# A planned two-layer attention kernel: V's weights split two blocks ahead, K's first weights split during Q in layer B's later units, and another model of loads and ports in the planner

## The chip, the cores and the metric

The kernel runs on one core of a Trainium2 chip. A core has a matrix engine (PE; PEld is its weight load), a vector engine (DVE), a scalar engine (ACT), a general engine (POOL), and SP, which here only issues transfers. They share an on-chip memory of 128 partitions; matrix products land in banks of 128 x 512 float32 values, which DVE or ACT must empty before PE can fill them again. Each engine works through its own queue in order and waits on semaphores for the others. The metric is the time of one launch in microseconds of device time.

## The reference

Two attention layers read inputs of their own, x of 2048 positions by 1024 features, with 32 heads of 32 features each:

```python
qkv = x @ wqkv                                     # both layers, 1024 -> 3 x 1024
# layer A: position s looks at s, s-2, s-4, ..., s-14 (8 keys, dilation 2)
logits = einsum("bhsd,bhswd->bhsw", q, kg) * Dh ** -0.5
# layer B: position s looks at the 256 positions s-255 .. s
scores = einsum("bhqd,bhkd->bhqk", q, k) * (Dh ** -0.5)
out = softmax(masked scores) @ v                   # both
y = concatenate([outA @ A_wo, outB @ B_wo], axis=-1)
```

## The kernel before, in words

**Tiling.** The work is cut into eight units of 512 positions. Units 0 to 3 are layer B (in the code "dense", DU = 4 of them), units 4 to 7 layer A, whose positions are sorted into even and odd ones so that its keys lie side by side. A unit has eight blocks of four heads. For a block, `qk_items` projects Q (`t = 0`) and K (`t = 1`), each over eight slices k of the features; `v_items` projects V in three parts, a wide one of four blocks and two narrow ones of two (`VPARTS`), the wide one in steps n over the weight tiles; `o_items` does the output projection of the unit before, while the blocks run. Every product is done in three matmuls (`TERMS`), since each float32 operand is split into a rounded high part and a rest: x·w = hi·hi + hi·lo + lo·hi.

**Weights and activations.** `Stream` holds one list of all tiles of weights and activations in the order in which they are used. `load_to(n)` fetches tiles up to n into a few `raw` buffers (`raw<-wqk`, `raw<-wv`, `raw<-wo`, `raw<-xs`: transfers issued by POOL at L194), `split_to(n)` splits them: a cast of the high part (L249 on ACT or L252 on DVE) and two subtractions for the rest (L255, DVE). The result is a tile `w`, `x` or `r`; `wpool` has three buffers for `w`. A load beyond the first ones is deferred until a buffer is free by the planner's clock. Since POOL's queue is in order, a load that waits for its buffer holds up what stands behind it there.

**Attention of layer B.** The halves of Q and K of a block are written to `nat` (L597 and L601), and SP copies them (L621) into stacks `qst` and `kst`, which put high and low parts below each other, so that one matmul gives all terms. Pass one multiplies `s<-kst,qst` for the row maxima and sums; DVE (L1356) and ACT (L1361) drain these banks, of which there are four. A small product `s<-ident,hl` carries the row values into the stack. Pass two multiplies `s<-qst,kst`, ACT exponentiates into `pbuf` (L1441), POOL (L1420) or DVE (L1423) cuts off the mask, and `o<-pbuf,vbuf` sums the values. Layer A's window scores live in `band` and go through DVE (L1184 to L1214). The constants (masks, the identity `ident`) are made by POOL at the start (L455 to L481), in a function that is put off by `defer(0.0)`.

**The order.** The program runs once in Python as a planner: four lists, first passes, second passes, projections and helpers, are merged by which item is ready first by the class `Clock`, and the instructions are issued in this order. `Clock` keeps a free time for each engine (`use`, `start`), a model of the memory port that DVE and POOL share (`port`), and a model of when transfers land (`issue`, `move` with the costs in `MOVE`); `defer(t, f)` puts f off until the clock has come to t. So a changed cost issues no instruction but changes the places of many. The kernel has no loops on the chip.

Of the kernel before, what the change touches and what calls it, by code (L numbers as in the profile page):

```python
# [22 lines left out]
ASK = 2  # L23
# [35 lines left out]
BY_ACT = (0, 2)  # L59
# [3 lines left out]
class Clock:  # L63
# [4 lines left out]
    SEEN = dict(act=0.15, dve=0.115, pool=0.08)  # L68
    LEAD = dict(sp=1.34, act=0.97, pool=1.43)
    HOLD = dict(sp=0.63, act=0.35, pool=0.6)  # L70
    MOVE = dict(load=(2.12, 0.14), store=(0.64, 0.4), copy=(1.18, 0.56),
                halo_out=(0.4, 0.68), halo_in=(0.55, 0.6), halo_few=(0.28, 0.51),
                half=(0.8, 0.14), first=(1.4, 0.14), part=(0.33, 0.56))

    def __init__(self):
        self.free = dict(pe=0.0, act=0.0, dve=0.0, pool=0.0, sp=0.0)
        self.port = dict(dve=0.0, pool=0.0)
        self.later, self.lands, self.busy = [], [], []
        self.n = 0

    @property
# [3 lines left out]
    def start(self, eng, port, *ready):  # L85

        t = max((self.free[eng],) + ready)
        if eng == "pool":
            t = max(t + 0.06, self.port["dve"])
        elif port:  # L90
            t = max(t, self.port["pool"])
        return t

    def ends(self, eng, dur, *ready, port=False):
        return self.start(eng, port, *ready) + dur

    def use(self, eng, dur, *ready, port=False):
        end = self.free[eng] = self.ends(eng, dur, *ready, port=port)
        if eng == "pool" or port:
            self.port[eng] = end  # L100
        return end + self.SEEN[eng]

    def issue(self, eng, kind, *ready):
        start = max((self.free[eng],) + ready) + (0.28 if eng == "pool" else 0.0)
        self.free[eng] = start + self.HOLD[eng]
        return self.move(start + self.LEAD[eng], *self.MOVE[kind])

    def copy(self, kind, *ready):

# [13 lines left out]

        return self.lands[-8] if len(self.lands) >= 8 else 0.0

    def move(self, t, dur, tail):

        busy = self.busy = [x for x in self.busy if x[1] > self.now - 20.0]
        i = 0
        while i < len(busy):  # L130
            if busy[i][1] <= t or busy[i][0] < t:
                t = max(t, busy[i][1])
            elif busy[i][0] - t >= dur:
                break
            else:
                t = busy[i][1]
            i += 1
        busy.insert(i, (t, t + dur))
        return t + dur + tail

    def defer(self, t, f):
# [8 lines left out]
class Stream:  # L150
# [14 lines left out]
    def load_to(self, n):  # L165
        while not self.loaded:
            for i in range(3):
                self.raw[i] = self.raws.tile([P, 1024], F32, tag="raw", name="raw"), [None, None]
            for i, raw in enumerate(self.more):
                self.raw[3 + i] = raw, [None, None]  # L170
            for n, (i, h) in enumerate(FIRST):
                raw, t = self.raw[i]
                ap = self.items[i][1]
                queue, took = (self.nc.scalar, self.ck.load) if n in BY_ACT else (self.nc.sync, self.ck.copy)
                if h is None:
                    queue.dma_start(raw.rearrange("p (a b) -> p a b", a=2), ap)
                    t[:] = [took("first", self.ck.now)] * 2
                else:
                    queue.dma_start(raw[:, S * h:S * h + S], ap[:, h] if len(ap.shape) == 3 else ap[:, S * h:S * h + S])
                    t[h] = took("half", self.ck.now)  # L180
            self.loaded = 6
        self.wanted = max(self.wanted, n)
        while self.loaded < min(n, len(self.items)):
            gate = self.gates.get(self.loaded)
            if gate and not gate():
                return
            k = self.loaded - NRAW
            if self.loaded >= self.wide and (self.loaded - self.wide) % (2 * NRAW) < NRAW:
                raw = self.room()
            else:  # L190
                raw = self.more[k] if 0 <= k < len(self.more) else self.raws.tile([P, 1024], F32, tag="raw", name="raw")
            ap = self.items[self.loaded][1]
            early = k < len(self.more)
            (self.nc.scalar if early else self.nc.gpsimd).dma_start(raw if len(ap.shape) == 2 else raw.rearrange("p (a b) -> p a b", a=2), ap)  # L194
            self.raw[self.loaded] = raw, (self.ck.load if early else self.ck.fetch)("load", self.ck.now)
            self.loaded += 1
# [68 lines left out]
def kernel(ctx, tc, xs, wqk, wv, wo, outs, units):  # L265
# [274 lines left out]
    def qk_items(u, s):  # L540
# [14 lines left out]
        def evac_window(t, ps, bank):  # L555
            if t == 0:
                h2["qk"] = natp.tile([P, 2 * S + 16], F32R, tag="nat", name="nat").bitcast(F32)[:, :2 * S + 8]
                nc.scalar.activation(h2["qk"][:, :S], ps, AF.Copy, scale=SCALE)
                e = ck.use("act", 0.485, ck.now + ck.SEM)
                by_head(0, S, e)  # L560
            else:
                qk = h2["qk"]
                nc.scalar.copy(qk[:, S + 8:], ps)
                e = ck.use("act", 0.485, ck.now + ck.SEM)
                nc.scalar.copy(qk[:, S:S + 8], tails[:, s, :])
                e = ck.use("act", 0.2, e)
                if u + 1 < U and not units[u + 1][3]:
                    ck.defer(e + 1.0, lambda: (nc.vector.memset(tails[:, s, :], 0.0), ck.use("dve", 0.08, ck.now)))
                if u + 1 < U and units[u + 1][3]:
                    nc.scalar.copy(tails[:, s, :], ps[:, S - 8:])  # L570
                    e = ck.use("act", 0.2, e)
                by_head(S, 2 * S + 8, e)
            rg.give(bank, e)
# [65 lines left out]
        for t in range(2):  # L639
            h = {}  # L640

            def ready(k, t=t, h=h):
                if k == 0:
                    st.split_to(where["qk", u, s, t] + 1)
                    w = st.ready[where["qk", u, s, t]]
                    h["r"] = w if isinstance(w, list) else [w, w]
                    return latest(rg.when(), h["r"][0], xready[u][0])
                if k >= len(xready[u]):
                    return None
                if k == NK - 1 and nat + t >= NN and (dense or t == 0):  # L650
                    n = done["nat"].get(nat + t - NN)
                    return n and max(xready[u][k], n - 0.6)
                return max(xready[u][k], h["r"][k // 4])

            def run(k, t=t, h=h):
                if k == 0:
                    h["ps"], h["b"] = rg.take()
                    h["w"], _ = st.get(where["qk", u, s, t])
                for i, (a, b) in enumerate(TERMS):
                    mm(h["ps"], h["w"][:, a, k * P:(k + 1) * P], xt[u][k][:, b, :],  # L660
                                     start=(k == 0 and i == 0), stop=(k == NK - 1 and i == 2))
                then = where["qk", u, s, t] + 1
                if t == 1 and s == 0 and u:
                    then = max(then, st.split)
                kinds = [kind for kind, _ in st.items[then:then + 2]]
                if k == ASK and kinds and kinds[0] not in ("x", "xw"):
                    st.split_to(then + 1)
                if k == ASK and t == 0 and u > DU and kinds[:1] == ["x"] and st.split >= where["qk", u, s, 1]:
                    st.split_to(where["qk", u, s, 1] + 1)
                if kinds[:1] == ["xw"] and k in (0, 2, 4, 6):  # L670
                    st.split_to(then + 1 + k // 2)
                if kinds == ["w", "w"] and k == 5 and (then in firsts or then + 1 in firsts):
                    st.split_to(then + 2)
                if kinds == ["w", "xw"] and k == 6:
                    st.split_to(then + 2)
                if k in (4, 6) and kinds[:1] == ["xt"]:
                    st.split_to(then + k // 2)
                if k == 6 and t == 1 and not hg:
                    st.split_to(7)

            def after(k, t=t, h=h):
                if k == NK - 1:
                    evac(t, h["ps"], h["b"])

            for k in range(NK):
                out.append((lambda k=k, ready=ready: ready(k), lambda k=k, run=run: run(k), 3 * CG,
                            lambda k=k, after=after: after(k)))
# [12 lines left out]
    def v_items(u, part):  # L700
# [25 lines left out]
        def run(r, n, k, b):  # L726
# [15 lines left out]
            done_block = k == kw - 1 and b == 1  # L742
            if wide and r == 0:
                if k == 0 and b == 1 and n < 3:
                    ahead(item_of(n + 1))
            elif wide:
                if done_block and n == 0:
                    ahead(item_of(4))
# [5 lines left out]
        def ahead(i):  # L754
            if st.items[min(i, len(st.items) - 1)][0] != "x":
                st.split_to(i + 1)
# [894 lines left out]
```

## Time and profile before

| | before |
|---|---|
| median of three runs | 1803.32 us |
| lowest and highest of them | 1802.33 and 1803.51 us |
| the profiled execution | 1802.41 us |
| its span, from the first to the last instruction | 1800.7 us |
| granted clock of PE | 0.999 |

The busy times of the page are sums over the instructions of an engine. A row of the timeline gives the start, the time of a run of like instructions, the engine, the line, the operation with its output and inputs, their count, and in brackets how long the engine was idle before it and on what it waited. A row of the waits gives who waited at which line for whom, the total, how often, and the longest. Line numbers in these rows are of the kernel before.

### The profile page before, as it was taken

What the parts mean: (1) busy time and instruction counts of PE and PEld (TensorE: products, weight loads), DVE (VectorE), ACT (ScalarE), POOL (GpSimd) and SP (SyncE); (2) the same over time, 40 slices, a digit from 0 to 9 for tenths busy, and PEclk for the clock granted to TensorE, in tenths of its full rate; (3) what the DMA queues carried; (4) which work ended last, traced back from release to release, by engine and by line L of the source; (5) the groups of instructions that cost most, each with busy time, mean ns of one, the idle gap of its engine ahead of it and who ended that gap; (6) DMA issues with size and microseconds to landing.
All of it is one profiled execution on the core that took longest, in us unless ns stands there. A gap on an engine that the chain in (4) does not pass through costs nothing.

```text
span 1800.7 us, 38453 instructions
## 1 busy us (share of the span) xinstructions
PE 1775.3 (99%) x14496; PEld 1439.2 (80%) x14496; DVE 1297.4 (72%) x2887; ACT 940.3 (52%) x2336; POOL 413.7 (23%) x952
## 2 busy tenths in 40 slices
PE   9999999999999999999999999999999999999999
PEld 7787777888777888778788778877888787778887
DVE  6777876768867769867678566756666768688866
ACT  4565566555656565655655444534454435355442
POOL 3222323222242222332223400110011101001120
PEclk9999999999999999999999999999999999999999
DMA  8354664644645555455546265665466558758984
GB/s 245 112 152 135 185 167 135 171 138 138 185 141 172 152 131 167 144 159 148 141 124 174 84 190 180 213 211 187 160 212 204 192 177 285 265 181 273 350 287 146
DMA packets 154794, 324.58 MB, mean 180 GB/s; under 512 B 18032, under 2 KB 58992, under 8 KB 154608
## 3 DMA queue, kind: packets, MB, share of 16 engines
q0 software_dynamic: 45792, 166.74, 29.8%
q1 hardware_dynamic: 98736, 137.02, 26.6%
q10 hardware_dynamic: 10080, 18.35, 2.7%
q8 instruction: 115, 1.88, 0.4%
q14 instruction: 71, 0.58, 0.1%
HBM read 201.33 MB, written 53.48 MB: 142 GB/s over the span
## 4 chain that ended last, share of the span: by engine, by line
PE 87%; DVE 5%; issue 3%; DMA 2%; ACT 2%; POOL 1%; DVEq 0%; POOLq 0%; ACTq 0%
PE g L297 68%; PE s L297 13%; PE o L297 6%; DMA raw<-xs 1%; DVE w L255 1%; DVE x L255 1%; ACT s L1361 0%; DVE band L1212 0%; DMA raw<-wv 0%; DVE sm L1208 0%; DVE band L1184 0%; ACT w L249 0%; DMA raw<-wqk 0%; DVE w L252 0%; DMA qst<-nat 0%
## 5 line engine op out<-in xcount | busy, mean ns | idle before, releaser
L297 PE MATMUL g<-x,w 128*128 128x512 f32 x3552 | 878.9, 393 | 5.0 <-DVE x L255 3.9
L297 PEld LDWEIGHTS g<-x,w 128*128 128x128 f32 x3552 | 654.8, 188 | 135.2 <-issue 6.6
L255 DVE TENSOR_TENSOR w<-raw,w 128x512 fp32r<-128x512 f32 x510 | 334.3, 697 | 48.5 <-ACT w L249 42.4
L1361 ACT ACTIVATE s<-s,nm 128x384 f32<-128x384 f32 (+2 forms) x512 | 274.4, 537 | 108.2 <-DVE nm L1356 101.7
L1356 DVE CUSTOM_DVE_ANT_0 s<-s,mask_d 128x384 f32<-128x384 f32 (+2 forms) x512 | 261.7, 553 | 91.7 <-PE s L297 91.4
L297 PE MATMUL g<-w,x 128*128 128x256 f32 (+1 forms) x1728 | 307.9, 327 | 2.4 <-DVE w L255 1.5
L1420 POOL TENSOR_SCALAR_AFFINE_SELECT pbuf<-pbuf 128x128 f32<-128x128 f32 (+1 forms) x603 | 218.4, 390 | 317.9 <-ACT pbuf L1441 315.9
L297 PEld LDWEIGHTS g<-w,x 128*128 128x128 f32 x1728 | 255.2, 190 | 28.0 <-DVE w L255 2.8
L297 PE MATMUL g<-r,w 128*128 128x512 f32 x960 | 239.0, 393 | 1.7 <-issue 1.2
L1441 ACT ACTIVATE pbuf<-s 128x384 f32<-128x384 f32 (+2 forms) x480 | 203.1, 505 | 64.2 <-PE s L297 62.0
L297 PEld LDWEIGHTS g<-r,w 128*128 128x128 f32 x960 | 177.2, 188 | 37.2 <-issue 2.0
L194 POOL DMA_DIRECT2D raw<-wqk x126 | 68.6, 544 | 407.4 <-DVE w L255 256.8
L297 PEld LDWEIGHTS s<-qst,kst 128*128 128x128 f32 x704 | 113.4, 188 | 42.6 <-ACT s L1361 16.8
L297 PE MATMUL s<-kst,qst 96*128 96x384 f32 (+2 forms) x512 | 142.6, 342 | 0.9 <-ACT s L1361 0.7
L297 PE MATMUL s<-qst,kst 128*128 128x256 f32 (+2 forms) x704 | 137.0, 302 | 4.0 <-ACT s L1361 3.2
L252 DVE CAST w<-raw 128x1024 fp32r<-128x1024 f32 x173 | 119.8, 692 | 19.3 <-PE g L297 9.0
L249 ACT CAST w<-raw 128x1024 fp32r<-128x1024 f32 (+1 forms) x83 | 85.8, 1038 | 71.1 <-PE g L297 29.7
L297 PEld LDWEIGHTS s<-kst,qst 96*128 96x128 f32 x512 | 93.6, 189 | 26.3 <-issue 4.4
L1361 ACT ACTIVATION_READ_ACCUMULATOR s<-s,nm 128x1 f32 x512 | 105.3, 206 | 0.0
L1223 ACT COPY wide<-band 32x512 f32<-32x512 f32 x128 | 79.0, 617 | 31.0 <-DVE band L1214 29.4
L297 PE MATMUL o<-pbuf,vbuf 128*32 128x384 f32 (+2 forms) x1408 | 91.2, 388 | 0.0
L597 ACT ACTIVATE nat<-g 128x512 fp32r<-128x512 f32 x64 | 38.3, 598 | 98.2 <-PE g L297 89.0
(90 smaller groups left out, 1432.1 us busy)
## 6 DMA issues: line engine op xcount, KB each, us to landing
raw<-wqk POOLq DMA_DIRECT2D x126, 512.0 KB, 4.6
raw<-wv POOLq DMA_DIRECT2D x60, 512.0 KB, 5.0
qst<-nat SPq DMA_DIRECT2D x96, 256.0 KB, 5.7
kst<-nat SPq DMA_DIRECT2D x96, 256.0 KB, 5.7
raw<-wo POOLq DMA_DIRECT2D x44, 512.0 KB, 4.4
raw<-xs POOLq DMA_DIRECT2D x28, 512.0 KB, 4.5
outs<-ost ACTq DMA_DIRECT2D x38, 256.0 KB, 3.1
kst<-halo SPq DMA_DIRECT2D x72, 128.0 KB, 4.5
```

Of the source, the lines that this page charges most:

```text
L194: (self.nc.scalar if early else self.nc.gpsimd).dma_start(raw if len(ap.shape) == 2 else raw.rearrange("p (a b) -> p a b", a=2), ap)
L249: nc.scalar.copy(t[:, 0, :], raw)
L252: nc.vector.tensor_copy(t[:, 0, :], raw)
L255: nc.vector.tensor_tensor(t[:, 1, c:c + 512], raw[:, c:c + 512], t[:, 0, c:c + 512].bitcast(F32), op=ALU.subtract)
L297: nc.tensor.matmul(out, left, right, **k)
L597: nc.scalar.activation(hl[:, 0, :], ps, AF.Copy, scale=sc)
L1223: nc.scalar.copy(diag[r:r + 32, :, :, c:c + 32], turned[r:r + 32, :, :, 1, :])
L1356: nc.vector.tensor_tensor_reduce(ps[:, :n], ps[:, :n], mask[:, cut:full], scale=-1.0, scalar=BIG, op0=ALU.add, op1=ALU.min, accum_out=nm)
L1361: nc.scalar.activation(ps[:, :n], ps[:, :n], AF.Exp, bias=nm, scale=-1.0, accum_out=sm)
L1420: nc.gpsimd.affine_select(w, w, pattern=[[0, m], [step, n]], compare_op=ALU.is_ge, fill=0.0, base=base, channel_multiplier=chan)
L1441: nc.scalar.activation(w, ps[:, :pack * n].rearrange("p (j n) -> p j n", j=pack), AF.Exp)
```

## The change

1. `Clock.MOVE`: a load is now costed as 1.5 us of transfer and 0.76 us until it is seen, before 2.12 and 0.14.
2. `Clock.start` and `use`: a POOL instruction waits, in the model, only for a port interval of DVE that holds its start (the list `held`), before for the end of DVE's last one.
3. `Clock.move`: the transfers of POOL's queue and those of SP's and ACT's queues are two lines in the model, each in order, which run at half speed while both are at work; before, every transfer took the first free gap of one line.
4. `Stream.load_to`: the loop over the first transfers names its counter `turn`. Before, it was `n`, the function's argument, and left it at 8, so that the first call asked for two loads more than it was called for; these two then stood in POOL's queue ahead of the constants.
5. The clearing of `tails` (8 times, in unit 5) moves from DVE to POOL.
6. `qk_items`: K's first weights of a unit are asked for at slice `ASK` = 2 of Q where `u > 1` (units 2 to 7), before where `u > DU` (units 5 to 7).
7. `v_items`: in a wide part, step n asks for tile `min(n + 2, 3)`, before for n + 1.

```diff
-    MOVE = dict(load=(2.12, 0.14), store=(0.64, 0.4), copy=(1.18, 0.56),
+    MOVE = dict(load=(1.5, 0.76), store=(0.64, 0.4), copy=(1.18, 0.56),
...
         if eng == "pool":
-            t = max(t + 0.06, self.port["dve"])
-        elif port:
-            t = max(t, self.port["pool"])
-        return t
+            t += 0.06
+            return next((e for s, e in self.held if s <= t < e), t)
+        return max(t, self.port) if port else t
...
-        if eng == "pool" or port:
-            self.port[eng] = end
+        if eng == "pool":
+            self.port = end
+        elif port:
+            self.held = [x for x in self.held if x[1] > self.now - 5.0] + [(end - dur, end)]
...
-    def move(self, t, dur, tail):
-
-        busy = self.busy = [x for x in self.busy if x[1] > self.now - 20.0]
-        i = 0
-        while i < len(busy):
-            if busy[i][1] <= t or busy[i][0] < t:
-                t = max(t, busy[i][1])
-            elif busy[i][0] - t >= dur:
+    def move(self, eng, t, dur, tail):
+
+        mine, other = self.moves[eng == "pool"], self.moves[eng != "pool"]
+        t = begin = max(t, mine[-1][1] if mine else 0.0)
+        for s, e in other:
+            if e <= t:
+                continue
+            n = max(s - t, 0.0)
+            if n >= dur:
                 break
-            else:
-                t = busy[i][1]
-            i += 1
-        busy.insert(i, (t, t + dur))
+            t, dur = t + n, dur - n
+            n = min((e - t) / 2, dur)
+            t, dur = t + 2 * n, dur - n
+            if not dur:
+                break
+        mine.append((begin, t + dur))
+        del mine[:-40]
         return t + dur + tail
...
-            for n, (i, h) in enumerate(FIRST):
+            for turn, (i, h) in enumerate(FIRST):
...
-                    ck.defer(e + 1.0, lambda: (nc.vector.memset(tails[:, s, :], 0.0), ck.use("dve", 0.08, ck.now)))
+                    ck.defer(e + 1.0, lambda: (nc.gpsimd.memset(tails[:, s, :], 0.0), ck.use("pool", 0.08, ck.now)))
...
-                if k == ASK and t == 0 and u > DU and kinds[:1] == ["x"] and st.split >= where["qk", u, s, 1]:
+                if k == ASK and t == 0 and u > 1 and kinds[:1] == ["x"] and st.split >= where["qk", u, s, 1]:
                     st.split_to(where["qk", u, s, 1] + 1)
...
                 if k == 0 and b == 1 and n < 3:
-                    ahead(item_of(n + 1))
+                    ahead(item_of(min(n + 2, 3)))
```

The lines of the changed kernel are numbered 5 higher than those of before in the parts shown here. The instructions are the same in kind and number but for part 5; what changes is their order. Four places follow.

POOL's queue at the start, before (`raw<-wqk` and `raw<-wv` are loads, the others the constants):

```order
L194 DMA raw<-wqk 128x1024 x2
L463 MEMSET keep_d 128x128
L464 ISA
L464 AFFINE_SELECT ident<-keep_d 128x128
...
L457 AFFINE_SELECT keep_d<-keep_d 128x128
L194 DMA raw<-wv 128x2x512 x5
```

and of the changed kernel:

```order
L468 MEMSET keep_d 128x128
L469 ISA
L469 AFFINE_SELECT ident<-keep_d 128x128
...
L462 AFFINE_SELECT keep_d<-keep_d 128x128
L199 DMA raw<-wqk 128x1024 x2
L199 DMA raw<-wv 128x2x512 x5
```

The two loads have moved behind the constants.

DVE's queue where the first K weights of unit 2 are split, before (`s,nm` are first passes, `pbuf,keep` masks of second passes):

```order
L1356 ISA nm 128x1
L1423 TENSOR_TENSOR pbuf<-pbuf,keep_d 128x128
L1423 TENSOR_TENSOR pbuf<-pbuf,keep_f 128x128
L1423 TENSOR_TENSOR pbuf<-pbuf,keep_d 128x128
L1423 TENSOR_TENSOR pbuf<-pbuf,keep_f 128x128
L252 CAST w<-raw 128x1024
L255 TENSOR_TENSOR w<-raw,w 128x512 x2
L601 SCALAR_TENSOR_TENSOR nat<-g,nat 128x512
```

and of the changed kernel:

```order
L1325 TENSOR_TENSOR r<-o,r 128x512
L1361 ISA s,nm<-s,mask_d 128x384
L1361 ISA nm 128x1
L257 CAST w<-raw 128x1024
L260 TENSOR_TENSOR w<-raw,w 128x512 x2
L1361 ISA s,nm<-s,mask_d 128x384
L1361 ISA nm 128x1
```

The split has moved from behind the masks of the second pass to among the first passes of that block.

DVE's queue at unit 7's activations, before (`band` is layer A's window, `r<-g` belongs to the output projection):

```order
L1208 TENSOR_REDUCE sm<-band 128x16
L1210 RECIPROCAL sm<-sm 128x16
L1212 TENSOR_TENSOR band<-band,sm 128x16x40
L1214 STREAM_TRANSPOSE band<-band 128x1024
L1184 TENSOR_TENSOR band<-s,near 128x4x40 x4
L255 TENSOR_TENSOR x<-raw,x 128x512 x2
L979 TENSOR_TENSOR r<-g,r 128x512 x2
L255 TENSOR_TENSOR w<-raw,w 128x512 x2
```

and of the changed kernel:

```order
L1219 STREAM_TRANSPOSE band<-band 128x1024
L984 TENSOR_TENSOR r<-g,r 128x512 x2
L260 TENSOR_TENSOR x<-raw,x 128x512 x2
L984 TENSOR_TENSOR r<-g,r 128x512 x2
L260 TENSOR_TENSOR x<-raw,x 128x512 x2
L1189 TENSOR_TENSOR band<-s,near 128x4x40 x4
L984 TENSOR_TENSOR r<-g,r 128x512 x2
L260 TENSOR_TENSOR w<-raw,w 128x512 x2
```

The last `x` split of the unit now stands ahead of the masks `band<-s,near`.

PE's queue in layer B from the end of a block's K (the last `g<-x,w`) to the block's first scores, before (the stacks with `_129` and `_127` are the block's own, those ahead of them belong to the block before):

```order
L297 MATMUL g<-x,w 128x512 x9
L297 MATMUL s<-kst_130,qst_128 128x384
L297 MATMUL g<-r,w 128x512 x6
L297 MATMUL s<-kst_130,qst_128 128x384
L297 MATMUL g<-r,w 128x512 x3
L297 MATMUL s<-kst_130,qst_128 128x384 x2
L297 MATMUL g<-r,w 128x512 x24
L297 MATMUL s<-ident,hl 32x128
L297 MATMUL g<-r,w 128x512 x9
L297 MATMUL s<-kst_129,qst_127 128x384 x3
```

and of the changed kernel (`_125`, `_123`):

```order
L302 MATMUL g<-x,w 128x512 x12
L302 MATMUL g<-r,w 128x512 x18
L302 MATMUL s<-ident,hl 32x128
L302 MATMUL g<-r,w 128x512 x15
L302 MATMUL s<-kst_125,qst_123 128x384 x4
```

Between K's end and the first scores there are 33 products `g<-r,w` where there were 42, and no scores of the block before.

More of the change, by code (lines that the diff above doesn't have):

```diff
@@ L76, in __init__ @@
         self.free = dict(pe=0.0, act=0.0, dve=0.0, pool=0.0, sp=0.0)
-        self.port = dict(dve=0.0, pool=0.0)
-        self.later, self.lands, self.busy = [], [], []
+        self.port, self.held = 0.0, []
+        self.later, self.lands, self.moves = [], [], [[], []]
         self.n = 0
@@ L105, in issue @@
         self.free[eng] = start + self.HOLD[eng]
-        return self.move(start + self.LEAD[eng], *self.MOVE[kind])
+        return self.move(eng, start + self.LEAD[eng], *self.MOVE[kind])
     def copy(self, kind, *ready):
@@ L170, in load_to @@
                 self.raw[3 + i] = raw, [None, None]
-            for n, (i, h) in enumerate(FIRST):
+            for turn, (i, h) in enumerate(FIRST):
                 raw, t = self.raw[i]
                 ap = self.items[i][1]
-                queue, took = (self.nc.scalar, self.ck.load) if n in BY_ACT else (self.nc.sync, self.ck.copy)
+                queue, took = (self.nc.scalar, self.ck.load) if turn in BY_ACT else (self.nc.sync, self.ck.copy)
                 if h is None:
```

## The prediction

> **What bounds the kernel now.** I read the page's busy times first, then the waits of TensorE (PE), then the timeline around each long one.
>
> ```profile
> span 1800.7 us, 38453 instructions
> PE 1775.3 (99%) x14496; PEld 1439.2 (80%) x14496; DVE 1297.4 (72%) x2887; ACT 940.3 (52%) x2336; POOL 413.7 (23%) x952
> ```
> PE is the bound: 25.4 us of its span are idle, and the diff leaves its matmuls alone. So the change can win only from that remainder, and can lose without such a limit. Of the waits of PE (total us, times, longest) these bear on it:
>
> ```profile
> PE s L297 <- ACT s L1361: 4.6, 7, 1.0
> PE g L297 <- DVE x L255: 3.9, 3, 2.8
> PE g L297 <- DVE w L255: 3.0, 6, 0.8
> PE s L297 <- issue: 2.2, 1, 2.2
> PE s L297 <- DVE hl L1382: 0.6, 2, 0.3
> PE g L297 <- DVE r L1320: 0.4, 2, 0.2
> ```
> No wait is long; they are small misses of one split (a cast at L252, a subtraction at L255) or one bank. A bracket understates its loss, since a matmul record is longer than its cadence:
>
> ```profile
> 862.08 2.22 PE L297 MATMUL g<-x,w 128*128 128x512 f32 x9
> 866.95 5.64 PE L297 MATMUL g<-r,w 128*128 128x512 f32 x24
> 872.49 2.31 PE L297 MATMUL g<-r,w 128*128 128x512 f32 x9
> 874.64 0.69 PE L297 MATMUL s<-kst,qst 96*128 96x384 f32 x3
> ```
> The first two rows differ by 15 matmuls of one size and 3.42 us, 0.228 us each; a run of nine then leaves 2.22 − 8 × 0.228 = 0.40 for its last record. So PE loses about 0.17 us beside each bracket, and I add it. In the last two rows PE goes from output-projection work (`g<-r,w`) to the first scores of a block; they come up again below.
>
> **The start.** Before, two weight loads stand ahead of the constants in POOL's queue, and the first waits for a buffer:
>
> ```profile
> 8.70 0.68 POOL L194 DMA_DIRECT2D raw<-wqk  x1 [8.19 <-DVE x L255]
> 10.45 0.22 POOL L463 MEMSET keep_d<- 128x128 f32 x1
> 10.74 3.83 POOL L464 TENSOR_SCALAR_AFFINE_SELECT ident<-keep_d 128x128 fp32r<-128x128 f32 x1
> 22.93 1.47 POOL L194 DMA_DIRECT2D raw<-wv  x2
> 14.46 1.29 DVE L255 TENSOR_TENSOR w<-raw,w 128x512 fp32r<-128x512 f32 x2
> 19.69 2.88 PE L297 MATMUL g<-x,w 128*128 128x512 f32 x12
> 30.55 0.69 DVE L252 CAST w<-raw 128x1024 fp32r<-128x1024 f32 x1 [7.10 <-DMA raw<-wv]
> 31.30 0.50 PE L297 MATMUL g<-w,x 128*128 128x512 f32 x1 [0.56 <-DVE w L252]
> 32.63 0.50 PE L297 MATMUL g<-w,x 128*128 128x512 f32 x1 [0.83 <-DVE w L255]
> ```
> The constants take 22.93 − 10.45 = 12.5 us. After, they begin where POOL's idle time now begins, 8.70 − 8.19 = 0.5, and end by 13.0; the loads follow at some 0.7 each: the two of wqk at 13.0 and 13.7, V's first at 14.4 instead of 22.93. That is 8 us against a DVE wait of 7.1, so both PE waits on V's weights go: 0.56 + 0.83 + 2 × 0.17 = **−1.7**. The price is the first wqk load, 4.3 us later. The page's medians from issue to landing (last column):
>
> ```profile
> raw<-wqk POOLq DMA_DIRECT2D x126, 512.0 KB, 4.6
> kst<-nat SPq DMA_DIRECT2D x96, 256.0 KB, 5.7
> ```
> 13.0 + 4.6 = 17.6; a cast (0.69) and the first subtraction (0.65) make 18.9, where PE wants it at 19.69. That is close: I take **+0.3**, between 0 and 1.5. Nothing behind it on DVE is due sooner.
>
> [...] In the row at 14.46 two such subtractions beside POOL's constants still took 1.29 us, while it was POOL whose select took 3.83; here POOL lost. [...]
>
> **V's weights two blocks ahead.** This only moves two DVE (or ACT) splits of each wide V part ahead by one block, 2 to 4 us of PE's work, at units 0 to 5. Where V waits outside the start:
>
> ```profile
> 208.99 0.44 PE L297 MATMUL s<-kst,qst 96*128 96x384 f32 x1 [0.73 <-ACT s L1361]
> 1174.34 0.50 PE L297 MATMUL g<-w,x 128*128 128x512 f32 x1 [0.38 <-DVE w L255]
> ```
> The second is one late weight and goes (**−0.55**). The first is a score bank among V's work; the moved splits clear its DVE queue (**−0.9**; it may stay). The earlier split also holds a `wpool` buffer longer; three buffers and PE consuming one per two to four us leave room.
>
> **K's first weights during Q, units 2 to 4.** Before, they are split after Q has ended, behind four mask multiplications, and the score banks that ACT and DVE drain come late:
>
> ```profile
> 451.81 0.69 DVE L252 CAST w<-raw 128x1024 fp32r<-128x1024 f32 x1
> 452.53 1.29 DVE L255 TENSOR_TENSOR w<-raw,w 128x512 fp32r<-128x512 f32 x2
> 453.14 0.33 PE L297 MATMUL s<-qst,kst 128*128 128x128 f32 x1 [0.61 <-ACT s L1361]
> 709.29 0.33 PE L297 MATMUL s<-qst,kst 128*128 128x128 f32 x1 [0.61 <-ACT s L1361]
> 965.36 0.33 PE L297 MATMUL s<-qst,kst 128*128 128x128 f32 x1 [0.61 <-ACT s L1361]
> 461.72 0.22 PE L297 MATMUL s<-ident,hl 128*32 128x128 f32 x1 [0.31 <-DVE hl L1382]
> ```
> With the weights ready, PE has K's product to put between those scores: 3 × (0.61 + 0.17) = **−2.3**. The operands of `ident`, late twice (row above and the waits' "0.6, 2"), are then asked for further ahead: 2 × 0.48 = **−1.0**. What covers the moved 2 us of DVE work is the gap between Q's scores; if that cover is gone, a bank is late by up to 1.3 us there, three times.
>
> **The new model of loads, ports and queues.** MOVE, `move` and `held` issue nothing; they alter the order. Two effects I could tie to rows. The `r` subtractions late twice (0.4 in all) gain some 9 us of lead: **−0.8**. And unit 7's activations:
>
> ```profile
> 1517.17 0.81 DVE L1208 TENSOR_REDUCE sm<-band 128x16 f32<-128x640 f32 x1
> 1521.22 1.27 DVE L255 TENSOR_TENSOR x<-raw,x 128x512 fp32r<-128x512 f32 x2
> 1521.95 1.88 PE L297 MATMUL g<-x,w 128*128 128x512 f32 x7 [2.78 <-DVE x L255]
> 1524.35 0.50 PE L297 MATMUL g<-x,w 128*128 128x512 f32 x1 [0.52 <-DVE w L255]
> ```
> Between 1517.17 and 1521.22 DVE does the window's softmax and masks, 4.05 us, while PE starves. In the new order the x split stands ahead of the masks and its load is asked for 3.8 us of PE work sooner: 2.78 + 0.52 + 2 × 0.17 = **−3.6**. Next late would be the softmax itself, which feeds scores much further on. The memsets of `tails` (8, on POOL now, each at most the 0.22 of the row at 10.45) lie beside other work: 0.
>
> What is lost. The K copies of eight blocks of layer B come nearer to their first scores. In the block at 864 before, K ends at 864.3 (862.08 + 2.22) and 42 `g<-r,w` stand before the scores at 874.64; after, 33, so 33 × 0.229 + 0.06 = 7.6 us. The copies:
>
> ```profile
> L621 SPq DMA_DIRECT2D kst<-nat x3: 546/562/594, 865.0 to 866.2; - x3
> DMA to landing us min/median/max: 6.8/7.0/7.2
> ```
> landed at 866.2 + 7.2 = 873.4, 9.1 after K's end: 1.5 short. This block landed slowly; with the 5.7 of the page it lands at 871.9 and just holds. I take one such miss, **+1.5**, between 0 and 8 × 1.5 = 12. Layer A keeps nearly its order, but one load is asked for 2.7 us of PE work later:
>
> ```profile
> 1402.74 0.53 POOL L194 DMA_DIRECT2D raw<-tv  x1 [5.03 <-DVE r L255]
> ```
> Its split came 2.2 us after it landed, so **+0.5** (0 to 2.7). And where order changes elsewhere, small misses will open as the old order had them (25.4 us in all); I expect few, **+2** (0 to 6, a quarter of the old idle time).
>
> **Sum.** −1.7 −0.55 −0.9 −2.3 −1.0 −0.8 −3.6 = −10.9; +0.3 +1.5 +0.5 +2 = +4.3; net −6.6. Against the profiled execution, 1802.4 us (its span 1800.7 and 1.7 around it), that is 1795.8; the median 1803.3 stands 0.9 above that execution, so **1796.7**. A measurement of this kernel tells about 0.2%, 3.6 us, from no change.
>
> **Rivals.**
> 1. The waits only move. The bank at 453 is drained no faster and shows itself a few scores on, as do the ident, r, 1174 and 209 waits: 2.3 + 1.0 + 0.8 + 0.55 + 0.9 = 5.6 come back, 1802.3. For it: ACT's seven score waits have no common cause. Against: the 1522 and start waits have plain ones.
> 2. Slower: the K copies. They share the DMA engines with POOL's loads, now asked for sooner. At 22 to 35 us, where both queues were full, they took longer:
>
> ```profile
> raw<-wv POOLq DMA_DIRECT2D x4, 512.0 KB, 8.0
> kst<-nat SPq DMA_DIRECT2D x3, 256.0 KB, 7.7
> ```
> At 7.7 the miss is 866.2 + 7.7 − 864.3 − 7.6 = 2.0 a block, 16 in eight, 14.5 more than I took: 1811. It ends slower once a block loses over (6.6 + 1.5 + 3.6) / 8 = 1.5. Against it: the copies' median over the kernel is 5.7, which just holds. [...]
> 3. All gains, no new misses: only +0.3 and +0.5 lost, 1793.2. For it: each gain above has its own row. Against: a new order without a single new miss.
> 4. The constants hold up the start's subtractions, which they now run beside: at most by one select as long as the 3.83 of 10.74, 1800.5. Against it: the 1.29 of 14.46, and the first subtractions come after the first of the constants. [...]
>
> **Chances.** Forecast 0.48 (its own range 1793 to 1800), rival 1 0.19, rival 2 0.16, rival 3 0.13, rival 4 0.04. The bound of 0.2% puts "faster" below 1799.7: the forecast but for 0.03 of its upper end, and rival 3: 0.58. Same: rivals 1 and 4 and that end, less 0.01: 0.25. Slower: rival 2 and mixtures past 1806.9: 0.17. The range 1792 to 1808 holds the forecast and rivals 1, 3 and 4, and leaves out rival 2.
>
> **What would show it.** Right: no V-weight wait near 31, no DMA wait of 7 us on DVE there; no score wait where 453, 709 and 965 had one; no x wait near 1520. Wrong: a wait of PE on a DMA of `kst` or `qst` (the trace of before has none); a wait at about 19.7 for the first wqk; subtractions before 10 us longer than 0.69; score waits on ACT more than 4.6 in total; or "issue" waits (2.2 now), which I cannot place, moving by 2.

## The result, and the profile after

The changed kernel takes 1817.42 us (median of six runs, 1813.95 to 1821.67), the kernel before 1803.41 (six runs, 1802.33 to 1807.71). The ratio is 1.0071, with a 95% interval from 1.0055 to 1.0088: slower by 0.7%, where 1796.7 and a range of 1792 to 1808 were forecast.

The first lines of the page of after:

```profile
span 1815.0 us, 38450 instructions
PE 1782.7 (98%) x14496; PEld 1443.0 (80%) x14496; DVE 1296.3 (71%) x2866; ACT 939.4 (52%) x2331; POOL 422.3 (23%) x978
kst<-nat SPq DMA_DIRECT2D x96, 256.0 KB, 4.5
```

PE does the same matmuls, so the 14.3 us of span are time that it lost. I had written that the instructions are the same in kind and number but for part 5. They are not: DVE's count went from 2887 to 2866, ACT's from 2336 to 2331, POOL's from 952 to 978. The planner also chooses by its clock which engine does a mask or a cast; of POOL's 26 more, 8 are the memsets and 18 are masks of second passes (L1425, 621 after 603). The waits of PE of after (total us, times, longest):

```profile
PE s L302 <- ACT s L1366: 6.3, 8, 2.1
PE g L302 <- DVE band L879: 5.2, 2, 3.7
PE g L302 <- DVE w L260: 2.6, 5, 1.1
PE g L302 <- DVE w L257: 1.6, 1, 1.6
PE g L302 <- ACT w L254: 1.6, 2, 1.4
...
PE g L302 <- DVE x L260: 1.3, 2, 1.1
PE s L302 <- DMA halo<-nat: 1.2, 1, 1.2
...
PE s L302 <- DVE hl L1387: 0.6, 1, 0.6
```

The x wait of 2.8 has gone; in its place stand longer waits for score banks and a new one, the output products' additions (L879). All waits of PE together grew from 20.7 us to 26.1, 5.4 of the 14.3. PE's whole idle time grew by 6.9 (25.4 to 32.3), so 1.5 lie in gaps too small for this list. The other 7.4 are busy time: the clock takes 3.4 of them (last section), and what lengthened the matmul records by the other 4.0 was not traced.

To see where, I compared the times at which the two traces reach equal amounts of PE's own work (each matmul counted by its cadence). Gain or loss by stretch, in us; the heads are times of before, and "products" are the last output products:

| | 2–59 | 59–249 | 249–536 | 536–797 | 797–1055 | layer A, –1652 | products, –1702 | to the end |
|---|---|---|---|---|---|---|---|---|
| after | −2.9 | +0.2 | +2.7 | +2.9 | +3.9 | −1.1 | +8.5 | 0.0 |

The entries hang on the cadence that one gives to a matmul; another choice moves single ones by up to 1.6 us. The start gains, as forecast. Each of the stretches that hold the start of unit 2, 3 or 4 (near 456, 717 and 978) loses about 3, and the last products lose 8.5.

**One unit's start.** In the timelines of after at the start of unit 4, DVE, ACT and PE in turn:

```profile
965.32 0.43 DVE L257 CAST x<-raw 128x512 fp32r<-128x512 f32 x1 [4.29 <-PE g L302]
968.05 0.56 DVE L1361 CUSTOM_DVE_ANT_0 s<-s,mask_d 128x384 f32<-128x384 f32 x1
```
```profile
968.70 0.56 ACT L1366 ACTIVATE s<-s,nm 128x384 f32<-128x384 f32 x1 [2.85 <-DVE nm L1361]
```
```profile
961.50 0.34 PE L302 MATMUL s<-kst,qst 96*128 96x384 f32 x1
969.42 0.45 PE L302 MATMUL s<-kst,qst 96*128 96x384 f32 x1 [2.14 <-ACT s L1366]
```

PE wrote a score bank at 961.50. DVE could have drained it at once, but at the head of its queue stood the cast of an activation for the next unit, whose buffer PE was still reading: 4.29 us. Behind it the drain of the scores came at 968.05, ACT's at 968.70, and PE stood 2.14 us until ACT had freed a bank.

**The last products.** SP, DVE and PE of after:

```profile
1647.71 7.89 SPq L1105 DMA_DIRECT2D r<-od  x2
```
```profile
1663.63 2.87 DVE L1110 TENSOR_TENSOR r<-r 128x512 f32<-128x512 f32 x4 [4.63 <-DMA r<-od]
1680.50 0.69 DVE L879 TENSOR_TENSOR band<-g,r 128x512 f32<-128x512 f32 x1 [2.67 <-DMA outs<-band]
```
```profile
1671.85 5.79 PE L302 MATMUL g<-x,w 128*128 128x512 f32 x24 [1.49 <-DVE band L879]
1681.34 5.28 PE L302 MATMUL g<-x,w 128*128 128x512 f32 x15 [3.71 <-DVE band L879]
```

It is the same shape. The half sums (L1110) stand at DVE's head 4.63 us before their operands have landed; the additions that empty PE's banks, and the stores whose buffers the next ones need, come later by that.

The waits of DVE tell it in sum. Before, DVE waited nowhere for `r<-od` or `raw<-xs` (ACT's casts waited for `raw<-xs`, 18.6 us before and 23.2 after); after:

```profile
DVE r L1110 <- DMA r<-od: 9.1, 3, 4.6
...
DVE x L257 <- DMA raw<-xs: 4.5, 3, 2.9
DVE x L257 <- PE g L302: 4.3, 1, 4.3
```

### The profile page after: what moved, and what is told of

Read it like the earlier page. It is cut to its first block, busy times and chain, and to the rows that moved or that the text cites. A ratio compares the mean times of both kernels' runs of the same rounds, so it can differ in the third digit from the quotient of the medians.

```text
span 1815.0 us, 38450 instructions
## 1 busy us (share of the span) xinstructions
PE 1782.7 (98%) x14496; PEld 1443.0 (80%) x14496; DVE 1296.3 (71%) x2866; ACT 939.4 (52%) x2331; POOL 422.3 (23%) x978
## 4 chain that ended last, share of the span: by engine, by line
PE 83%; DVE 7%; DMA 6%; issue 2%; ACT 2%; POOL 1%; SPq 0%; ACTq 0%; DVEq 0%; POOLq 0%
PE g L302 66%; PE s L302 12%; PE o L302 6%; DMA raw<-xs 2%; DVE w L260 2%; DVE s L1361 1%; DMA r<-od 1%; DMA od<-r 1%; DMA raw<-tv 1%; DVE x L260 1%; DVE w L257 1%; ACT s L1366 1%; POOL pbuf L1425 1%; DMA outs<-band 0%; ACT w L254 0%
## 5 line engine op out<-in xcount | busy, mean ns | idle before, releaser
L1425 POOL TENSOR_SCALAR_AFFINE_SELECT pbuf<-pbuf 128x128 f32<-128x128 f32 (+1 forms) x621 | 229.9, 398 | 269.6 <-ACT pbuf L1446 267.2
L199 POOL DMA_DIRECT2D raw<-wv x60 | 38.7, 645 | 237.5 <-DVE w L260 124.6
```

The lines of the kernel that those rows point to most:

```text
L1425: nc.gpsimd.affine_select(w, w, pattern=[[0, m], [step, n]], compare_op=ALU.is_ge, fill=0.0, base=base, channel_multiplier=chan)
```

## The experiments

Theory 1, formed from the two places above: the new models let the planner put work on DVE ahead of its data, and cause the loss. Theory 2: the early split of K's first weights causes most of it, at the units' starts.

Times are medians in us, ratios are to runs of before beside them (1803.0 to 1803.9). Part numbers are those of the change.

### Each part alone

The kernel before, with part 4, 6, 7, or parts 1 to 3:

```diff
# a_turn
-            for n, (i, h) in enumerate(FIRST):
+            for turn, (i, h) in enumerate(FIRST):
# a_kf
-                if k == ASK and t == 0 and u > DU and ...
+                if k == ASK and t == 0 and u > 1 and ...
# a_va
-                    ahead(item_of(n + 1))
+                    ahead(item_of(min(n + 2, 3)))
# a_models: MOVE's load, start and use, move, as in the change
```

> The kernel before with part 4 alone (the loop counter is called turn, so POOL makes the constants ahead of the two loads). Theory 1 (the new models of loads, transfers and ports cause the loss; the other parts are about free) and theory 2 (K's first weights during Q cause most of it) agree here: the start gains what it gained in the changed kernel, 2.8 us by PE's 50th us of work, so about 1800.6. If the start's gain needs V's weights two blocks ahead as well, it stays near 1803.

> The kernel before with part 6 alone (K's first weights during Q where u > 1). Theory 1: within 2 us of before, 1801 to 1805, and no wait of a score bank on ACT over 1 us near 456 to 475, 705 to 730 and 969 to 990. Theory 2: the three unit starts lose as in the changed kernel, 2.5 + 3.6 + 3.5 = 9.6, so about 1813.

> The kernel before with part 7 alone (V's weights two blocks ahead). Both theories: within 2 us of before; the wait of 0.38 at 1174 goes. If V's splits crowd DVE's queue at the unit starts (a wait for w of 1.1 us at 727 in the changed kernel), 2 to 5 us slower.

> The kernel before with parts 1, 2 and 3 alone (cost of a load, ports, two lines of transfers). Theory 1: the whole loss and no gain at the start, 1803 + 14 + 3 = about 1820, with DVE waiting for r<-od and PE for a bank of the output products (L879 in the changed kernel) between 1650 and 1710. Theory 2: the loss of the tail alone, 11 us, about 1814, and nothing at 456, 705 and 969.

| | time | ratio, interval | 2–59 | 59–249 | 249–536 | 536–797 | 797–1055 | –1652 | –1702 |
|---|---|---|---|---|---|---|---|---|---|
| a_turn | 1803.03 | 0.9997, 0.9988–1.0007 | −1.8 | +0.1 | 0.0 | +0.2 | 0.0 | +3.2 | −0.1 |
| a_kf | 1803.66 | 0.9999, 0.9990–1.0009 | −0.8 | +0.1 | +2.6 | +5.2 | +0.2 | −6.4 | −0.3 |
| a_va | 1808.72 | 1.0025, 1.0016–1.0034 | +0.3 | +0.2 | +2.1 | +1.7 | +0.9 | +1.6 | −0.3 |
| a_models | 1822.24 | 1.0105, 1.0087–1.0124 | +2.2 | +2.8 | +3.0 | +3.1 | +5.2 | −5.7 | +5.4 |

The stretches are of one profiled execution each, the times medians. In a_turn the queues of PE, DVE and ACT are those of before, so its +3.2 is what one execution can differ by in a stretch. a_models' products hang most on the cadence: they lie between +1.9 and +5.4. a_turn missed its 1800.6: its start gains 1.8, and its median shows no gain clear of noise.

Theory 1 has its main point: the models cost the most, 18 us, mostly at the same places as in the changed kernel, and theory 2's 1813 for a_kf did not come. It is wrong that the rest is free. V's two blocks ahead, which were to gain, lose 4.8. Twice, where a unit's output projection begins, PE waits 0.8 us for ACT's cast of `r` (the rest of the 4.8 was not traced):

```profile
521.95 0.51 PE L297 MATMUL g<-r,w 128*128 128x512 f32 x1 [0.78 <-ACT r L1316]
```

K's first weights cost nothing in the sum, but not because they do nothing. In a_kf the bank waits of 453 and 709 have gone, and the operands of `ident` are late instead, at nearly the same place in units 2 and 3:

```profile
460.27 0.69 DVE L1320 TENSOR_TENSOR r<-o,r 128x512 fp32r<-128x512 f32 x1 [1.31 <-ACT r L1316]
461.65 0.17 DVE L1379 TENSOR_TENSOR nl<-nm,ln 128x16 f32<-128x16 f32 x1 [0.69 <-ACT ln L1374]
```
```profile
462.39 0.28 PE L297 MATMUL s<-ident,hl 128*32 128x128 f32 x1 [2.86 <-DVE hl L1382]
722.18 0.29 PE L297 MATMUL s<-ident,hl 128*32 128x128 f32 x1 [2.87 <-DVE hl L1382]
```

0.61 + 0.31 us of waits became 2.86, twice. What it wins back lies behind unit 4, where two waits on "issue" are gone that are gone in a_u4 too (below).

### The models one by one, and the change without them

The kernel before with part 3, part 2 or part 1 alone; and the changed kernel with parts 1 to 3 undone. The expectation of a_move counts rows of PE's queue that differ from before; its counts were those of the first rows only. Over the whole queue, with runs of like matmuls as rows, the traces have 1048 of before's 1568 rows at another place for part 3, 905 for part 2 and 702 for part 1.

> The kernel before with part 3 alone (POOL's transfers and the others' as two lines at half speed). Theory 1a: this is the part of the models that loses, since of the three it moves the most rows of PE's queue (88 against 36 for the ports and none for the load's cost): 1815 to 1822, with the waits of score banks at the starts of units 2, 3 and 4 and of the output products near 1690. Theory 1b: the loss needs the load's smaller cost too; then within 4 us of 1804.

> The kernel before with part 2 alone (a POOL instruction waits only for a port interval that holds its start). Theory 1a: within 3 us of 1804. Rival: the ports decide where DVE's and POOL's masks and splits stand, and with them the banks; then 5 us or more of the models' 18 show here, 1809 or more.

> The kernel before with part 1 alone (a load costs 1.5 + 0.76 in the model, before 2.12 + 0.14: the same sum, a shorter hold of the line). If a model that lets loads through too soon makes DVE wait at its head: 5 us or more slower, 1809 or more. If part 1 only offsets part 3: within 3 us of 1804.

> The changed kernel with parts 1, 2 and 3 undone, so the kernel before with the loop counter, the memsets, K's first weights and V's two blocks. If the parts add up: 1804 - 0.9 - 0.3 + 4.8, about 1807.5, and the models cost the changed kernel some 10 us. If V's weights need the new load model to be there in time, more: 1812.

a_move 1842.22 (1.0215, 1.0199–1.0230), a_port 1819.71 (1.0086, 1.0071–1.0101), a_load 1824.62 (1.0124, 1.0103–1.0146), no_models 1805.14 (1.0011, 1.0002–1.0021).

So no single model is the cause: each alone costs 16 to 39 us, all three 18. a_move lies 20 us above its range, and a_port misses theory 1a. Part 3 loses most with the old load. Parts 1 and 3 offset each other in part: together, with the rest of the change, they cost 17 (no_port, below, against no_models), less than a_move or a_load alone. Without the models the rest of the change costs 1.8 us, below both cases of its expectation, where the single parts sum to −0.9 − 0.3 + 4.8 = 3.6 (part 5 was not run alone). So 12.3 of the changed kernel's 14 us come with the models.

Whether each model loses by the same mechanism is only partly shown. DVE's waits on `r<-od` are 10.4 us in a_move and 11.2 in a_models; those on `raw<-xs` 8.7 in a_port and 9.1 in a_models. In a_load both are small (1.5 and 0.5), and its loss, with 39.6 us of PE waits of many kinds, stays without an explanation. One wait at DVE's head there is of the same kind, though: 10.1 us at 1380 for a `w` buffer that PE still read, where before's longest is 4.0. What it cost was not tried. The profiled executions of a_port and a_load are the longest of their runs (1827.66 and 1832.68).

### Single parts taken out of the changed kernel

The edits of a_port, a_kf and a_va, backwards.

> The changed kernel with part 2 undone (POOL waits in the model for DVE's last port interval, as before). Theory P: the port model is what loses, alone it cost 16; without it the changed kernel comes to 1804 to 1808. Rival: parts 1 and 3 lose by themselves (part 3 alone cost 39, with the dearer load), and the three models do not add up: 1814 or more.

> The changed kernel with part 6 undone. Alone, part 6 made the operands of ident late by 2.9 us at 462 and at 722 and yet cost nothing in the sum. If it is what loses at the starts of units 2 to 4 here (2.5 + 3.6 + 3.5 us): 1808. If x's splits, which stand ahead of their data, lose there: 1815 to 1819.

> The changed kernel with part 7 undone. Alone, part 7 cost 4.8 us. If that adds up: about 1812.6. If the new models give V's earlier splits their place, as part 7 and the models were made together: 1817 to 1821.

no_port 1822.53 (1.0109, 1.0095–1.0123), no_kf 1819.79 (1.0097, 1.0081–1.0112), no_va 1819.75 (1.0095, 1.0080–1.0111). Taking any one of them out wins nothing, not even V's two blocks, which cost 4.8 in the old order. no_port is 5 us slower than the changed kernel; no_kf and no_va are 2 us slower, but their intervals overlap that of the changed kernel (1.0055–1.0088). All three are misses of "the parts add up", and of theory P; the second cases came out, no_kf's but for 0.8 us.

### DVE's head of queue: the half sums and the activations

If DVE stands at work whose data is not there, that work must be placed later. Two constants of the planner do only that.

```diff
# t_slack: the changed kernel
-BG_REST, BG_SLACK, BG_EARLY = 2.0, 1.5, 8.0
+BG_REST, BG_SLACK, BG_EARLY = 2.0, 6.0, 8.0
# t_xat: t_slack, and
-XAT = 1
+XAT = 3
```

> The changed kernel, with the additions of the half sums planned 6.0 us instead of 1.5 us after the planner's landing of their operands (BG_SLACK). Theory of the tail: DVE stands 9.1 us at L1110 for r<-od in the changed kernel, with the outputs' additions and the bank of PE behind it; with the later place that wait goes and the 10 us between 1650 and 1710 with it, about 1807. Rival: the transfers are full there (busy share 0.9 to 1.0), so the sums only come later and PE waits for the loads of the products instead: 1815 to 1825.

> The changed kernel with the later half sums (t_slack, 1810.5) and the next unit's activations asked for two steps later in V (XAT = 3). If x's splits at DVE's head cause the losses at units 3 and 4 (there DVE waits 2.9 us for a load of xs and 4.3 us for PE to free a buffer, with score banks behind): 5 us less than t_slack, 1804 to 1806. If not: 1810 or more, since x is then later for Q.

t_slack: 1810.52 (1.0041, 1.0027–1.0054), 6.9 us less than the changed kernel. PE's queue keeps its order but for two rows and 17 rows of DVE's differ, so little else can have brought it; the products' stretch lost 2.7 instead of 8.5. The wait at the place of 1663.63 is nearly gone (DVE's waits between 1640 and 1712, after and t_slack; then PE of t_slack):

```profile
DVE r L1110 <- DMA r<-od: 8.1, 2, 4.6
```
```profile
DVE r L1110 <- DMA r<-od: 0.9, 1, 0.9
```
```profile
1671.57 5.28 PE L302 MATMUL g<-x,w 128*128 128x512 f32 x22 [1.12 <-DVE w L260]
1677.80 5.05 PE L302 MATMUL g<-x,w 128*128 128x512 f32 x21 [0.94 <-DVE band L879]
```

Its expectation of 1807 was 3.5 too good: a w split is late next. t_xat: 1805.97 (1.0007, 0.9997–1.0018), 4.5 less again, within the expected 1804 to 1806. At unit 4's start the casts of x no longer wait, and PE waits 0.25 us instead of 2.14; DVE, then PE of t_xat:

```profile
961.90 0.52 DVE L257 CAST x<-raw 128x512 fp32r<-128x512 f32 x1
```
```profile
967.37 0.80 PE L302 MATMUL s<-kst,qst 96*128 96x384 f32 x3
882.88 0.45 PE L302 MATMUL s<-qst,kst 128*128 128x384 f32 x1 [2.06 <-ACT pbuf L1446]
```

The last row is a wait that this order opened anew. At unit 3's start the casts are not cured; DVE of t_xat:

```profile
702.45 0.43 DVE L257 CAST x<-raw 128x512 fp32r<-128x512 f32 x1 [6.17 <-DMA raw<-xs]
```

In the three stretches with the starts of units 2, 3 and 4 t_xat still loses 1.4, 2.3 and about 5 us, where the changed kernel loses 2.7, 2.9 and 3.9. XAT also moves 381 of PE's 1523 rows, so that another order may have brought part of the gain. Together the two constants took back 11.4 of the 14 us. The mechanism is shown for the products, and for the wait at unit 4's start; for the other starts, and for the rest of what t_xat gains, it is argued.

> The changed kernel with each load planned to land 1.0 us later, its hold of the line unchanged: load=(1.5, 1.76). If landings taken too early are the cause: DVE's waits on DMA at its head (r<-od 9.1, raw<-xs 4.5 in the changed kernel) shrink and half of the 14 us or more come back, 1810 or less. If any new order loses as much, whatever its slack, since the numbers around it were fitted to the old one: 1815 to 1825.

```diff
# t_late: the changed kernel
-load=(1.5, 0.76)
+load=(1.5, 1.76)
```

t_late: 1815.20 (1.0062, 1.0049–1.0076). A general allowance of 1 us a load gives back 2.2, which the intervals do not tell from nothing, and not 7: its second case. DVE's waits did shrink, `r<-od` from 9.1 to 5.0 and `raw<-xs` from 4.5 to 1.8. One microsecond does not cover the 4.63 that was missing at one place; the longest wait for `r<-od` is still 3.4.

### What is worth keeping

```diff
# a_u4: the kernel before; t_u4: a_turn; t_all: t_xat
-  u > DU (t_all: u > 1) and kinds[:1] == ["x"]
+  u > 3 and kinds[:1] == ["x"]
```

> The kernel before with part 4 and with K's first weights during Q from unit 4 on (u > 3). In a_kf unit 4 gained 1.2 us and units 2 and 3 lost 2.7 and 4.5; part 4 gave 0.9. If they add up: 1801 to 1802, faster than both; if it is within the spread of before's order: 1803 to 1805.

> The kernel before with K's first weights during Q from unit 4 on (u > 3) and nothing else. If t_u4's gain is unit 4's split: 1798 to 1799.5, the 0.9 of part 4 missing. If both are needed: 1802 or more.

> t_xat (the changed kernel, half sums and activations placed later, 1806.0) with K's first weights during Q from unit 4 on only (u > 3). If K's early split loses in units 2 and 3 in every order, as in a_kf (2.7 and 4.5 us): 1800 to 1802. If under the new models it helps, as no_kf says (2.4 us slower without it): 1806 to 1809.

t_u4 1797.40 (0.9961, 0.9950–0.9973), a_u4 1797.65 (0.9969, 0.9959–0.9979), t_all 1807.68 (1.0025, 1.0014–1.0036). Asking for K's first weights during Q in unit 4 as well pays 5 to 7 us, which is faster than both kernels and some 4 us better than either case of t_u4; part 4 adds nothing that can be told apart there. In units 2 and 3 the same edit takes all of that back (a_kf against a_u4: 5 to 6). Under the new models it does not: t_all is no better than t_xat, as its second case said.

In the trace of a_u4 the bank wait of 965 is gone, 1.1 us by 978, of which 0.8 is given back by 1055; most, 4.6, comes in layer A, where two waits of PE on "issue" (2.2 and 1.2) are gone; 1.7 of the 4.6 is a fall of the clock (last section) that before has at 1436 and a_u4 at 171. Before, a run of 128 small score products broke off after 119; in a_u4 it does not (PE, before, then a_u4):

```profile
1054.36 1.24 PE L297 MATMUL s<-pbuf 32*32 32x40 f32 x119
1057.76 0.28 PE L297 MATMUL s<-pbuf 32*32 32x40 f32 x9 [2.17 <-issue]
```
```profile
1053.11 1.31 PE L297 MATMUL s<-pbuf 32*32 32x40 f32 x128
```

"issue" says only that PE waited there for nothing that the profile shows; what held it, and why the moved rows avoid it, was not tried.

## Why the prediction was wrong, step by step

- **The failing step is "+2 (0 to 6)" for the misses of a new order.** I took them as a quarter of the old order's idle time. The stretches with the starts of units 2 to 4 lost 9.5 and the products 8.5; 12.3 us came with the models (no_models), and 6.9 from half sums that stood at DVE's head ahead of their data (t_slack). Every order made with a changed model lost 11 or more, unless it was given t_slack's allowance. My reading, which t_slack supports for one constant, is that the old idle time was what is left of an order whose constants had been fitted to it; it says nothing of one that has not. One of the signs of being wrong that I had named came: score waits on ACT of 6.3, above 4.6. I listed rivals as single mechanisms with a row of before behind each, and these waits had no row of before.
- **Start (−1.7, +0.3):** right in its mechanism, too small in size. V's waits at 31 and 33 are gone, 2.9 us gained by 59 us, 1.8 with part 4 alone, where I had 1.4. The constants were done by 9.95, where I had 13.0, and the first wqk load came in time: PE began with it at 19.64, before at 19.69. POOL, then PE of after:

```profile
1.08 0.29 POOL L469 TENSOR_SCALAR_AFFINE_SELECT ident<-keep_d 128x128 fp32r<-128x128 f32 x1
9.95 1.23 POOL L199 DMA_DIRECT2D raw<-wqk  x2
```
```profile
19.64 2.88 PE L302 MATMUL g<-x,w 128*128 128x512 f32 x12
```

- **V two blocks ahead (−0.55, −0.9):** the late weight at 1174 is gone, the bank wait near 209 stayed (at 205). Alone the part costs 4.8 (a_va), in the changed order taking it out wins nothing (no_va). I gave the moved splits a free place on DVE and ACT without naming whom they pass: ACT's cast of `r` is one of them.
- **K's first weights (−2.3, −1.0):** the cover that I named, the gap between Q's scores, was not there in units 2 and 3. I priced its absence at a bank late by 1.3; it was `ident` late by 2.9 (a_kf). In the changed kernel waits for banks stand there still, 0.78 at 709 and 2.14 at 969, the latter behind x's cast. In unit 4 alone (a_u4) the bank wait went, as the step says, but for little; that a_u4 gains 5 to 7 us is luck by this step, since most of it comes in layer A.
- **`r` (−0.8) and 1522 (−3.6):** both waits are gone. But "next late would be the softmax" was wrong; it was a weight, 1.62 us at 1533.91, and of 3.6 about nothing was left (about −3 between 1500 and 1530 of before's time and +3 between 1530 and 1560, 1.7 of it the clock).
- **K copies (+1.5; rival 2):** right in size by luck: one wait of 1.2, at unit 2's start, put down to `halo<-nat` (in t_slack, where PE's order is the same but for two rows, to `kst<-nat`), and none in the other blocks. Rival 2 ended on the right side by the wrong mechanism: the copies' median fell from 5.7 to 4.5.
- **The `tv` load (+0.5, 0 to 2.7):** right in its mechanism. POOL issued it at 1410.15, before at 1402.74, ACT's cast waited for it, and PE then 1.45 us at 1415.86; ACT of after:

```profile
1414.76 1.04 ACT L254 CAST w<-raw 128x1024 fp32r<-128x1024 f32 x1 [2.30 <-DMA raw<-tv]
```

- **Rival 4:** POOL beside the start's subtractions cost them 0.05 to 0.15 us each, not a select's length.
- I had written that a model "issues nothing" and only moves the order. It moves work between engines too (18 masks), and this was the largest part of the change.

## What to carry to other kernels

When a change re-plans an in-order schedule, price the whole new order, not the waits that it removes: here most of the waiting rows that I priced had their remedy in the new order, and the loss came from rows that had not waited before. Look at what stands at the head of each in-order engine queue and ask whether its data, and the buffer that it writes, can be there by then; one early cast on DVE, 4.29 us ahead of its buffer, held up ACT, the score banks and PE. And when a planner's cost changes, try the slacks next to it as well: one of them, BG_SLACK, took back half of the loss here.

## What the runs showed of the hardware that was not expected

**A wait of PE costs more than its length, by 1.7 us, when the clock falls.** Granted clock in stretches of 4 us (the column after the busy times), of before, of after and of a_kf:

```profile
1436.00:1440.00 4.00, 4.00 (x39) 2.69 (x39) 1.82 (x3) 2.31 (x5) 1.23 (x3) 0.62 1.00 302
```
```profile
1680.00:1684.00 4.00, 2.66 (x9) 2.12 (x10) 3.40 (x6) 1.47 (x3) 0.00 (x0) 0.81 1.01 401
1684.00:1688.00 4.00, 4.00 (x49) 2.97 (x48) 4.00 (x7) 0.20 (x1) 1.06 (x2) 0.76 0.78 275
```
```profile
460.00:464.00 4.00, 1.61 (x5) 1.17 (x5) 2.50 (x7) 1.59 (x6) 0.00 (x0) 0.80 1.06 256
464.00:468.00 4.00, 4.00 (x19) 3.42 (x18) 3.77 (x6) 2.08 (x5) 1.12 (x2) 0.77 0.46 109
```

In after, (0.19 + 0.24) × 4 = 1.7 us are lost behind the wait of 3.71; in a_kf (0.20 + 0.23) × 4 = 1.7 behind that of 2.86. The traces hold such losses in steps of 1.7: one before, three after (5.1), nine's worth in a_move (15.4) and eight's in a_port (13.6). Not each wait does it: before, 2.78 us at 1522 left the clock at 1.00, while 0.97 and 0.77 in a row at 1434 brought it down. What decides it, no run here shows. The fall of the clock also goes with the wider spread of the slower kernels: the changed one's runs at granted clocks of 0.994 to 0.997 lie between 1821.67 and 1813.95, the longest at the lowest.

**A select of POOL lost far more beside DVE than DVE's subtractions beside selects.** The `ident` select, the one case shown, took 3.83 us beside DVE's subtractions before, and 0.29 after, when DVE had only a memset of 0.48 us under way. DVE's subtractions beside the constants were slightly longer in after's start than the 0.69 of before:

```profile
5.58 0.74 DVE L260 TENSOR_TENSOR x<-raw,x 128x512 fp32r<-128x512 f32 x1 [4.11 <-ACT x L254]
6.24 0.84 DVE L260 TENSOR_TENSOR w<-raw,w 128x512 fp32r<-128x512 f32 x1
```
